# A fused spectral filter and state-space kernel: weight rows loaded twice by one transfer, and a new order of work

## The chip, the cores and the metric

The kernel runs on one core of a Trainium2 chip. The metric is device time in microseconds (us), the median over runs; a second number, the span, is the time from the first to the last instruction of one profiled execution. Engines are named as in the profile: PE is the matrix engine (PEld its weight loads), DVE the vector engine, ACT the scalar engine, POOL the general-purpose engine. SP is a sequencer that here only issues transfers (DMAs); a transfer is carried out by 16 DMA engines.

## The reference, cut to what matters

```
g = sigmoid((x * gate_w).sum(-1))               # x: 2048 x 1024
X = rfft2(x);  X = X * (w_r + 1j * w_i)         # w: 2048 x 513 each
a = irfft2(X)                                   # the spectral half
dt = exp(log_dt);  Lb = exp(dt * Lambda)        # 1024 complex states
Bu = x @ (((Lb - 1) / Lambda)[:, None] * B).T
h[t] = Lb * h[t - 1] + Bu[t]                    # a scan over 2048 steps
b = 2 * Re(h @ C.T) + x * Dskip                 # the state-space half
out = g * a + (1 - g) * b
```

## The kernel before, in words

All transforms are matrix products. The work falls into five stages, and the products `psu` of the state-space half (512 matmuls of 128x512, line 774) are strewn between the spectral stages as filling.

1. **Start.** 16 row blocks of x are loaded (L340) and turned on PE (L375) into `xT`. `halves` adds and subtracts halves of xT on DVE into `xpm` (L393, L395).
2. **Stage 1**, 16 steps j. `fd` (L532) makes the transform along columns, ACT copies it to `X1` (L537); `s1` (L547, L548) makes half of the transform along rows, ACT copies it to `A1` (L551), and SP writes A1 to a scratch tensor in DRAM, `turn1` (L553). At most three A1 buffers exist, and one is free again when its write has landed.
3. **Stage 2**, 16 steps b. `s2w` reads `turn1` back in another order (`Bb`, L655), PE multiplies it by a small matrix (L665), ACT copies the result (L668). The weights for step b come straight from DRAM into `Z(b, 0)` and `Z(b, 1)`, real and imaginary, 128 partitions x 1024 each: 64 partitions are needed, and both halves of the partitions get the same 64 rows. So there are four weight transfers a step (L659), each of 64 partitions x 2 rows x 512 values. DVE multiplies in place (L670). Column 0 is special: POOL sets column 0 of Z(b, 1) to zero (L660) and ACT puts a corrected value into column 0 of Z(b, 0) (L672), made by `fixup` out of column 0 of stage 1 (a small transfer to DRAM and back, `Bcol`, L611). `is1` (L681, L682) is the inverse along rows; its result goes to the scratch tensor `turn2` (L686).
4. **Stage 3**, 16 steps bp. `is2` reads `turn2` back (`Cq`, L693) when all 16 writes have landed, `idft` (L716) finishes the inverse, and the gated result goes to DRAM (L722).
5. **Output**, 16 steps tb: `ps_y` (512 matmuls, L818, and 128 small ones, L825), DVE combines with the spectral half read back (L845), SP writes the result (L848).

Beside these, DVE rotates and scans the states (`rot`, L742 to L748, and L786); the tables for that come from ACT (`table`).

The weights live in two tensors, `wA` and `wB`, with room for four steps in all: the loads for step b + 4 wait until `is1` of step b has read its room. The first eight (real and imaginary of steps 0 to 3; 16 transfers before the change) are loaded long before stage 2.

**What sets the order.** Nothing in the program text is in its final order. Every operation is recorded with an engine, a key, a duration in us, and what it reads and writes (`plan.op`). `Plan.run` then walks through them with these durations: of the operations that could start next on an engine it takes the one of lowest key, and gives out buffers as it goes. What comes out is a fixed list for each engine, and each engine works through its list in order, waiting by semaphores. Keys and durations (the second argument of `pe`, `act`, `dve`, `pool`, and the arguments `us` and `issue` of `dma`) thus set only the order. All transfers of the spectral half are issued by SP, in its one list.

Transfers carry eight completion semaphores in rotation: in the built program each transfer waits, before it is issued, for the one issued eight places before it. So at most eight are under way.

Of the kernel before, what the change touches and what calls it, by code (L numbers as in the profile page):

```python
# [11 lines left out]
ACT = mybir.ActivationFunctionType  # L12
# [23 lines left out]
def _host_consts():  # L36
# [30 lines left out]
    uu = np.arange(64)[None, None, :]  # L67
# [178 lines left out]
def kernel(  # L246
# [81 lines left out]
    KX = [0.0, 6.0, 10.0, 14.0]  # L328
    A2 = nc.scalar.activation

# [8 lines left out]
    for r in range(16):  # L339
        dma(r, 0.68, lambda r=r: nc.sync.dma_start(out=xn.t[:, r, :], in_=x[P * r:P * (r + 1), :]), w=[(xn, r)])  # L340
# [9 lines left out]
    dma(16.1, 2.6, lambda: nc.sync.dma_start(out=G_all, in_=cst["G"].rearrange("p d k -> p (d k)")), w=[("G",)])  # L350
    for i in range(2):
        dma(16.2, 2.0, lambda i=i: nc.sync.dma_start(out=TF_sb[i].t, in_=cst["TF"][:, 8 * i:8 * (i + 1)]), w=[(TF_sb[i],)])
    dma(16.3, 1.0, lambda: nc.sync.dma_start(out=TK_sb, in_=cst["TK"]), w=[("TK",)])
# [28 lines left out]
    def turn_x(c):  # L382
        for q in range(4):
            r = 4 * c + q
            turn(KX[c] + q, lambda r=r: xn.t[:, r, :], (xn, r), lambda c=c, q=q: xT[c][:, :, P * q:P * (q + 1)],
                 ("xT", c, q), q % 2)
# [4 lines left out]
    def halves(c):  # L391
        lo, hi = xT[c][:, 0:4, :], xT[c][:, 4:8, :]
        dve(KX[c] + 8, 1.22, lambda: nc.vector.tensor_add(out=xpm.t[:, 0, :, TC * c:TC * (c + 1)], in0=lo, in1=hi),  # L393
            r=xT_of(c), w=[(xpm, c, 0)])
        dve(KX[c] + 8.5, 1.22, lambda: nc.vector.tensor_sub(out=xpm.t[:, 1, :, TC * c:TC * (c + 1)], in0=lo, in1=hi),  # L395
            r=xT_of(c), w=[(xpm, c, 1)])
# [98 lines left out]
    def table(jb, key):  # L495
        tt = tile_of([P, 2, TC], FP32, "tt", "tt")
        tf = tile_of([P, 2, TC], FP32, "tf", "tf")
        cs = tile_of([P, 2, TC], BF16, "cs", "cs")
        kk, rr = lambda: tt.t[:, 0, :], lambda: tt.t[:, 1, :]
        sn_f, cs_f = lambda: tf.t[:, 0, :], lambda: tf.t[:, 1, :]  # L500
        at = lambda v: v[:, jb:jb + 1]
        act(key, 0.72, lambda: A2(out=kk(), in_=tau_f, func=ACT.Identity, scale=at(thn), bias=MAGIC),
            r=[("tau",), ("tht0",)], w=[(tt, 0)])
        act(key, 0.63, lambda: A2(out=kk(), in_=kk(), func=ACT.Identity, bias=-MAGIC), r=[(tt, 0)], w=[(tt, 0)])
        dve(key, 0.75, lambda: nc.vector.scalar_tensor_tensor(out=rr(), in0=tau_f, scalar=at(thn), in1=kk(), op0=ALU.mult,
                                                             op1=ALU.subtract), r=[("tau",), ("tht0",), (tt, 0)], w=[(tt, 1)])
# [34 lines left out]
    def s1(j, X1, key):  # L541
# [11 lines left out]
        dma(key, 0.68, lambda: nc.sync.dma_start(out=turn1_dram[j], in_=A1.t), r=[(A1,)], w=[("t1", j)])  # L553
# [3 lines left out]
    W_v = [w.rearrange("(q b h) k -> b q h k", b=16, h=2) for w in (A_w_r, A_w_i)]  # L557
# [4 lines left out]
    Bcol, Qz = fx.tile([P, 2, 16], BF16, name="Bcol"), fx.tile([P, 2, 16], BF16, name="Qz")  # L562
# [40 lines left out]
    def fixup(key):  # L603
# [4 lines left out]
        for c in range(2):  # L608
            def f(c=c):
                with nc.allow_non_contiguous_dma(reason="tiny corner turn"):  # L610
                    nc.sync.dma_start(out=Bcol[:, c, :], in_=col0_v[c])  # L611
            dma(key, 0.4, f, r=[("col0",)], w=[("Bcol", c)])
# [40 lines left out]
    def s2w(b, key):  # L653
        Bb = tile_of([P, 2, K], BF16, "Bb", "Bb")
        dma(key - 6, 0.84, lambda: nc.sync.dma_start(out=Bb.t, in_=t1_v[b]), r=[("t1", j) for j in range(16)], w=[(Bb,)])  # L655
        wr = (home(b), b % 2)
        for i in range(2):
            for c in range(2):
                dma(key - 6, 0.5, lambda i=i, c=c: nc.sync.dma_start(out=Z(b, i)[64 * c:64 * (c + 1)], in_=W_v[i][b][:, :, 0:K]), w=[wr + (i, c)])  # L659
        pool(key - 4, 0.1, lambda: nc.gpsimd.memset(Z(b, 1)[:, :, 0:1], 0.0), w=[wr + (1, 0), wr + (1, 1)])  # L660
# [8 lines left out]
        for i in range(2):  # L669
            dve(key, 0.69, lambda i=i: nc.vector.tensor_mul(out=Z(b, i), in0=X2.t, in1=Z(b, i)),  # L670
                r=[(X2,)], w=[wr + (i, 0), wr + (i, 1)])
        act(key + 1, 0.2, lambda: nc.scalar.copy(out=Z(b, 0)[:, :, 0], in_=Qz.rearrange("p o b -> p (o b)")[:, 2 * b:2 * b + 2]),  # L672
            r=[("Qz",)], w=[wr + (0, 0), wr + (0, 1)])

    def is1(b, key):
# [7 lines left out]
        pe(key, 4 * U, f, r=[(home(b), b % 2, i, c) for i in range(2) for c in range(2)] + [(MI_sb[b // 8],)], w=[(psc,)])  # L683
        C1 = tile_of([P, 2, K], BF16, "C1", "C1")
        act(key, 1.01, lambda: nc.scalar.copy(out=C1.t, in_=psc.t), r=[(psc,)], w=[(C1,)])  # L685
        dma(key, 0.86, lambda: nc.sync.dma_start(out=turn2_dram[2 * b:2 * b + 2].rearrange("h p k -> p h k"), in_=C1.t), r=[(C1,)], w=[("t2", b)])  # L686

    t2_v = turn2_dram.rearrange("b (r g i) k -> i (b r) g k", r=4, g=2)
    ga_v = ga_dram.rearrange("(p b) n -> p b n", b=16)

    def is2(bp, key):
        Cq = tile_of([P, 2, K], BF16, "Cq", "Cq")
        dma(key - 6, 0.86, lambda: nc.sync.dma_start(out=Cq.t, in_=t2_v[bp]), r=[("t2", b) for b in range(16)], w=[(Cq,)])  # L693
# [14 lines left out]
    def idft(bp, ZT, key):  # L708
# [13 lines left out]
        dma(key, 0.75, lambda: nc.sync.dma_start(out=ga_v[:, bp, :], in_=eo.t.rearrange("p h k -> p (h k)")), r=[(eo,)], w=[("ga", bp)])  # L722
# [3 lines left out]
    def load_CT(n, key):  # L726
        pc, ri = divmod(n, 2)
        dma(key, 3.0, lambda: nc.sync.dma_start_transpose(
            out=CT[pc].t[:, ri], in_=(B_C_re, B_C_im)[ri][:, 2 * P * pc:2 * P * (pc + 1)]), r=[("step", 2 * n, 0)], w=[(CT[pc], ri)], issue=2.4)
# [28 lines left out]
    def load_BT(jb, key):  # L758
        BTb[jb] = tile_of([P, 2, 8, P], BF16, "BTs", "bt")
        for ri, src in enumerate((B_B_re, B_B_im)):  # L760
            dma(key, 1.45, lambda ri=ri, src=src: nc.sync.dma_start_transpose(
                out=BTb[jb].t[:, ri], in_=src[P * jb:P * (jb + 1), :]), w=[(BTb[jb], ri)], issue=1.28)
# [47 lines left out]
    def yout(tb, key, diag):  # L810
# [12 lines left out]
        def f():  # L823
# [5 lines left out]
        dma(key - 6, 0.75, lambda: nc.sync.dma_start(out=eo.t.rearrange("p h k -> p (h k)"), in_=ga_dram[P * tb:P * (tb + 1), :]),  # L829
            r=[("ga", bp) for bp in range(16)], w=[(eo,)])  # L830
# [20 lines left out]
    K_T0 = 9.21  # L851
    K_TB = 7.38
    K_D = 16.61
    K_O = 42.27
    K_TAB0 = 19.63
    K_TAB = 4.93
    K_F0 = 21.64
    K_F = 1.92
    K_W0 = 56.75
    K_W = 1.73  # L860
    K_WI = 1.97
    K_I0 = 14.79
# [19 lines left out]
    def turns_of(lo, hi):  # L882
        for p, (jb, pr) in list(enumerate(turns))[lo:hi]:
            if pr == 0:
                tabs[jb] = table(jb, K_TAB0 if jb == 0 else KB(p, 0) - K_TAB)
                if jb:
                    load_BT(jb, KB(max(p - 2, 0), 0) + 2)
            carries[jb] = bu(jb, pr, tabs[jb], carries.get(jb), (KB(p, 0), KB(p, 1)), KD(p))
            if pr == 0:
                rot_out(jb, 0, 1, KD(p) + K_O)  # L890
                rot_out(jb, 1, 1, 400 + 3 * jb)
            else:
                rot_out(jb, 2, 2, 430 + 3 * jb)
# [11 lines left out]
    dma(130, 1.4, lambda: nc.sync.dma_start(out=G_all[:, 0:4 * K], in_=cst["Gi"].rearrange("p r k -> p (r k)")), w=[("G",)])  # L905
# [15 lines left out]
    for tb in range(16):  # L921
        yout(tb, 400 + 7 * tb, diag)
# [32 lines left out]
```

## Time and profile before

| | |
|---|---|
| median of 3 runs | 351.77 us (351.68 to 352.96) |
| profiled execution, its own time | 352.5 us |
| its span | 350.7 us, PE clock granted 0.995 |
| PE busy | 331.2 us (94%), 1917 matmuls |
| DVE busy | 293.7 us (84%) |
| ACT busy | 193.5 us (55%) |
| POOL busy | 21.9 us (6%) |
| transfers | 55.77 MB, mean 159 GB/s |

A page of the profile gives busy time of each engine, the same in 40 slices of the span, the transfers by queue, the chain of work that ended last, and the costliest groups of instructions. A group line reads: line, engine, operation, output <- inputs, shape, count | busy us, mean ns of one | idle time of the engine before them, and who ended it. A timeline row reads: start, duration, engine, line, operation. In the transfer section, a queue's line gives packets, MB, and the time that the packets took as a share of 16 engines' time; the completion notes are counted among the packets.

### The profile page before, as it was taken

Reading aid. Unit: us, or ns where it says so; the run is one execution under the profiler, and the core shown is the slowest. Engines: PE = TensorE matmul, PEld = TensorE weight load, DVE = VectorE, ACT = ScalarE, POOL = GpSimd, SP = SyncE. Lnnn points to the kernel's source line nnn. Section 1 sums busy time; section 2 is a strip of 40 time slices with the busy share of each in tenths; the row PEclk is TensorE's granted clock in tenths of the full one; section 3 lists DMA queues with packets and bytes.
Section 4 is the critical chain, followed back from the end, with each engine's and each line's share of the span. In section 5 each row is a group of like instructions: output and inputs, shape, how many; then the busy total and the mean of one; then the engine's idle time right before and its main releaser. Section 6 shows DMA issues by size and latency. Waiting matters only on the chain.

```text
span 350.7 us, 5296 instructions
## 1 busy us (share of the span) xinstructions
PE 331.2 (94%) x1917; PEld 172.9 (49%) x1917; DVE 293.7 (84%) x476; ACT 193.5 (55%) x270; POOL 21.9 (6%) x63
## 2 busy tenths in 40 slices
PE   5999999999997797799899999999999999999995
PEld 4655554555553343344345766654544454444542
DVE  2979999899999787899899999999999999622331
ACT  3897999999997768777649997940000000000000
POOL 1080000000004600000000000000000000000000
PEclk9999999999999899999999999999999999999999
DMA  7998870461175868999997999985233104100001
GB/s 247 309 318 67 211 206 32 92 181 62 60 178 154 240 140 232 247 247 249 230 249 201 249 254 260 232 250 179 90 97 116 60 32 149 60 32 30 30 32 60
DMA packets 69346, 55.77 MB, mean 159 GB/s; under 512 B 39364, under 2 KB 56004, under 8 KB 69192
## 3 DMA queue, kind: packets, MB, share of 16 engines
q1 hardware_dynamic: 69048, 55.40, 58.0%
q0 software_dynamic: 192, 0.02, 1.7%
q8 instruction: 15, 0.25, 0.3%
q14 instruction: 11, 0.09, 0.1%
q10 hardware_dynamic: 80, 0.01, 0.0%
HBM read 30.75 MB, written 16.79 MB: 136 GB/s over the span
## 4 chain that ended last, share of the span: by engine, by line
PE 58%; DVE 16%; ACT 10%; DMA 9%; SPq 4%; issue 2%; DVEq 0%; POOL 0%; POOLq 0%; ACTq 0%
PE ps_y L818 32%; PE psu L774 13%; DVE h L786 5%; PE ps_id L716 3%; PE ps_fd L532 3%; DMA wB<-in_A_w_r_dram 3%; DMA xn<-in_A_x_dram 2%; PE ps_y L825 2%; DVE su L742 2%; ACT u L777 2%; PE pt L375 2%; SPq L659 2%; DMA h<-turn_scratch 1%; DVE wB L670 1%; ACT X L537 1%
## 5 line engine op out<-in xcount | busy, mean ns | idle before, releaser
L774 PE MATMUL psu<-xT,BTs 128*128 128x512 bf16 x512 | 117.0, 379 | 1.5 <-ACT h L685 1.2
L818 PE MATMUL ps_y<-CT,h 128*128 128x512 bf16 x512 | 113.7, 379 | 0.0
L774 PEld LDWEIGHTS <-BTs 128*128 128x128 bf16 x512 | 49.7, 98 | 59.0 <-issue 2.1
L818 PEld LDWEIGHTS <-h 128*128 128x128 bf16 x512 | 49.3, 98 | 56.6 <-DVE h L746 0.6
L786 DVE TENSOR_TENSOR_SCAN h<-r_sb,carry,u 128x512 bf16<-128x512 f32 x48 | 59.6, 1271 | 0.1
L845 DVE SCALAR_TENSOR_TENSOR o<-ps_y,omg,ga 128x1024 bf16<-128x1024 f32 (+1 forms) x17 | 20.6, 1219 | 32.2 <-PE ps_y L825 32.2
L777 ACT CAST u<-psu 128x1024 bf16<-128x1024 f32 x32 | 32.5, 1017 | 7.8 <-PE psu L774 4.7
L532 PE MATMUL ps_fd<-G_all,xpm 128*128 128x512 bf16 x128 | 30.1, 379 | 0.5 <-ACT A L551 0.5
L532 PEld LDWEIGHTS <-xpm 128*128 128x128 bf16 x128 | 18.6, 146 | 10.4 <-issue 0.7
L537 ACT CAST X<-ps_fd 128x1024 bf16<-128x1024 f32 x16 | 21.5, 1342 | 0.1
L742 DVE TENSOR_TENSOR su<-h,pn 128x1024 bf16<-128x1024 bf16 (+1 forms) x24 | 20.7, 863 | 0.2
L743 DVE TENSOR_TENSOR h<-h,pn 128x1024 bf16<-128x1024 bf16 (+1 forms) x24 | 20.7, 862 | 0.1
L742 DVE TENSOR_TENSOR su<-u,cs 128x2048 bf16<-128x2048 bf16 x16 | 19.4, 1214 | 0.3
L743 DVE TENSOR_TENSOR u<-u,cs 128x2048 bf16<-128x2048 bf16 x16 | 19.5, 1219 | 0.2
L786 DVE TENSOR_TENSOR_SCAN h<-r_sb,u 128x512 bf16<-128x512 f32 x16 | 19.1, 1212 | 0.0
L685 ACT CAST h<-ps_is 128x1024 bf16<-128x1024 f32 x16 | 16.2, 1016 | 2.4 <-PE ps_is L682 1.3
L670 DVE TENSOR_TENSOR wA<-h,wA 128x1024 bf16<-128x1024 bf16 x16 | 10.8, 695 | 7.2 <-ACT h L668 2.6
L551 ACT CAST A<-ps_s 128x1024 bf16<-128x1024 f32 x16 | 16.6, 1037 | 0.0
L668 ACT CAST h<-ps_s 128x1024 bf16<-128x1024 f32 x16 | 16.0, 1022 | 0.3 <-DMA turn_scratch<-h 0.3
L721 ACT ACTIVATE eo<-ps_id,gA 128x1024 bf16<-128x1024 f32 x12 | 13.4, 1153 | 1.4 <-PE ps_id L716 1.4
L716 PE MATMUL ps_id<-G_all,ZT 128*128 128x256 bf16 x104 | 13.0, 273 | 1.0 <-ACT ZT L704 1.0
L375 PE MATMUL pt<-ident,xn 128*128 128x128 bf16 x128 | 10.0, 243 | 4.0 <-DMA xn<-in_A_x_dram 3.9
(160 smaller groups left out, 397.6 us busy)
## 6 DMA issues: line engine op xcount, KB each, us to landing
xn<-in_A_x_dram SPq DMA_DIRECT2D x16, 256.0 KB, 5.3
turn_scratch<-A SPq DMA_DIRECT2D x16, 256.0 KB, 2.7
h<-turn_scratch SPq DMA_DIRECT2D x16, 256.0 KB, 4.1
turn_scratch<-h SPq DMA_DIRECT2D x16, 256.0 KB, 3.2
out_dram<-o SPq DMA_DIRECT2D x15, 256.0 KB, 2.0
ga_scratch<-eo SPq DMA_DIRECT2D x12, 256.0 KB, 2.8
eoc<-ga_scratch SPq DMA_DIRECT2D x12, 256.0 KB, 4.2
Cq<-turn_scratch SPq DMA_DIRECT2D x11, 256.0 KB, 4.3
```

What stands on the lines that cost most here:

```text
L375: nc.tensor.transpose(out=pt.t[:, j8, :], in_=src()[:, P * j8:P * (j8 + 1)], identity=ident)
L532: mm(pf.t[:, par].rearrange("p c k -> p (c k)"), lhsT=xA[:, par, db, j, :], rhs=G_sb[:, db, par, :], start=(db == 0), stop=(db == 3))
L537: act(key, 1.3, lambda: nc.scalar.copy(out=X1.t.rearrange("p c (k r) -> p r c k", r=2), in_=pf.t), r=[(pf, 0), (pf, 1)], w=[(X1,)])
L551: act(key, 1.01, lambda: nc.scalar.copy(out=A1.t, in_=psa.t), r=[(psa,)], w=[(A1,)])
L716: mm(pz.t[:, at, :], lhsT=ZT.t[:, 2 * par + half, c, :], rhs=Gi_sb[:, par, half, c, :], start=(half == 0), stop=(half == 1))
L742: dve(key, w, lambda: nc.vector.tensor_mul(out=sv(), in0=src()[:, ::-1], in1=bc(1)), r=sitem + [titem(1)], w=[(su,)])
L743: dve(key, w, lambda: nc.vector.tensor_mul(out=dst(), in0=src(), in1=bc(0)), r=sitem + [titem(0)], w=ditem)
L774: mm(psu.t[:, ri, :], lhsT=BT.t[:, ri, db, :], rhs=xT[c][:, db, :], start=(db == 0), stop=(db == 7))
L777: act(kb[cc], 1.01, lambda cc=cc, psu=psu: nc.scalar.copy(out=u.t[:, :, cc, :], in_=psu.t), r=[(psu, 0), (psu, 1)], w=ui(cc))
L786: dve(kd, 1.25, lambda cc=cc, ri=ri, carry=carry: nc.vector.tensor_tensor_scan(out=g()[:, ri, cc, :], data0=rb, data1=u.t[:, ri, cc, :], i ...
L818: mm(psy.t[:, 512 * dh:512 * (dh + 1)], lhsT=hbuf[jb // 4].t[:, jb % 4, ri, P * tb:P * (tb + 1)], rhs=CT[pc].t[:, ri, jb % 2, 512 * dh:512 ...
L845: dve(key - 1, 0.2 + 1.07e-3 * (b - a), lambda a=a, b=b: nc.vector.scalar_tensor_tensor(out=o.t[:, a:b], in0=psy.t[:, a:b], scalar=og, in1 ...
```

## The change

The numbers behind the names below are this diff's own lines.

1. **Weight loads.** The two halves of the partitions are filled by one transfer: the source is given a leading dimension of 2 with step 0 (`[:, None].to_broadcast`). Each of the 64 rows of the source is now two whole neighbouring weight rows, 2 x 513 values (2052 bytes), and the room for it grows by 2 values. `Z` reads 512 of each 513. Two transfers a step instead of four. In the built program the source pattern of one is 2 (step 0) x 64 x 1026 values, where it was 64 x 2 x 512; the destination is 128 partitions x 1026 values, where it was 64 x 2 x 512.
2. **Column 0.** `Qz` holds for every step the corrected value and a zero beside it, so one ACT copy fills column 0 of Z(b, 0) and Z(b, 1); the 16 POOL memsets go, one larger one is added.
3. **Turn buffer in read order.** `MI`'s columns are permuted, so that the two rows which a partition of `Cq` reads from `turn2` lie side by side: one run of 2048 bytes instead of two of 1024.
4. **Constant loads.** The load of the inverse table `Gi` comes after `Qz`; the second `MI` load names `Bcol` among its reads, which at that place of the program text orders the Bcol loads after it in the plan.
5. **Durations and keys.** Planned durations of transfers grow, and all keys change, so that the lists of all engines are new.

```diff
-    uu = np.arange(64)[None, None, :]
+    uu = np.arange(64).reshape(2, 2, 16).transpose(0, 2, 1).reshape(1, 1, 64)
...
-    KX = [0.0, 6.0, 10.0, 14.0]
+    K_T0 = -26.99
+    K_TB = 21.89
...
+    K_FIX = -256.65
...
+    K_GATE = 154.0
+    KX = lambda c: K_XP * (c > 0) + K_XS * max(c - 1, 0)
...
-    dma(16.1, 2.6, lambda: nc.sync.dma_start(out=G_all, in_=cst["G"].rearrange("p d k -> p (d k)")), w=[("G",)])
+    dma(16.1, 4.0, lambda: nc.sync.dma_start(out=G_all, in_=cst["G"].rearrange("p d k -> p (d k)")), w=[("G",)])
...
-    W_v = [w.rearrange("(q b h) k -> b q h k", b=16, h=2) for w in (A_w_r, A_w_i)]
+    W_v = [w.rearrange("(q b h) k -> b q (h k)", b=16, h=2)[:, None].to_broadcast([16, 2, 64, 2 * (K + 1)]) for w in (A_w_r, A_w_i)]
...
-    Bcol, Qz = fx.tile([P, 2, 16], BF16, name="Bcol"), fx.tile([P, 2, 16], BF16, name="Qz")
+    Bcol, Qz = fx.tile([P, 2, 16], BF16, name="Bcol"), fx.tile([P, 16, 2, 2], BF16, name="Qz")
...
-        act(key, 0.2, lambda: nc.scalar.copy(out=Qz, in_=qps.t), r=[(qps,)], w=[("Qz",)])
+        pool(60, 0.2, lambda: nc.gpsimd.memset(Qz[:, :, 1, :], 0.0), w=[("Qz", 1)])
+        act(key, 0.2, lambda: nc.scalar.copy(out=Qz[:, :, 0, :], in_=qps.t.rearrange("p o b -> p (o b)").rearrange("p (b h) -> p b h", h=2)),
+            r=[(qps,), ("Qz", 1)], w=[("Qz",)])
...
-    wA = tile_of([P, 4, 2, K], BF16, "wA", "b8")
-    wB = tile_of([P, 4, 2, K], BF16, "wB", "b8")
+    wA = tile_of([P, 4, 2 * (K + 1)], BF16, "wA", "b8")
+    wB = tile_of([P, 4, 2 * (K + 1)], BF16, "wB", "b8")
...
-        dma(30 + 16 * i, 2.0, lambda i=i: nc.sync.dma_start(out=MI_sb[i].t, in_=cst["MI"][:, 16 * i:16 * (i + 1)]), w=[(MI_sb[i],)])
+        dma(30 + 16 * i, 3.0, lambda i=i: nc.sync.dma_start(out=MI_sb[i].t, in_=cst["MI"][:, 16 * i:16 * (i + 1)]),
+            r=[("Bcol", 1)] if i else [], w=[(MI_sb[i],)])
...
-    Z = lambda b, i: home(b).t[:, 2 * (b % 2) + i]
+    Zs = lambda b: home(b).t.rearrange("p n (h k) -> p n h k", h=2)[:, 2 * (b % 2):2 * (b % 2) + 2, :, 0:K]
+    Z = lambda b, i: Zs(b)[:, i]
...
-        dma(key - 6, 0.84, lambda: nc.sync.dma_start(out=Bb.t, in_=t1_v[b]), r=[("t1", j) for j in range(16)], w=[(Bb,)])
+        dma(key - K_DM, 1.0, lambda: nc.sync.dma_start(out=Bb.t, in_=t1_v[b]), r=[("t1", j) for j in range(16)], w=[(Bb,)], issue=0.49)
...
-            for c in range(2):
-                dma(key - 6, 0.5, lambda i=i, c=c: nc.sync.dma_start(out=Z(b, i)[64 * c:64 * (c + 1)], in_=W_v[i][b][:, :, 0:K]), w=[wr + (i, c)])
-        pool(key - 4, 0.1, lambda: nc.gpsimd.memset(Z(b, 1)[:, :, 0:1], 0.0), w=[wr + (1, 0), wr + (1, 1)])
+            dma(key - K_DM, 1.05, lambda i=i: nc.sync.dma_start(out=home(b).t[:, 2 * (b % 2) + i], in_=W_v[i][b]), w=[wr + (i,)], issue=0.5)
...
-        act(key + 1, 0.2, lambda: nc.scalar.copy(out=Z(b, 0)[:, :, 0], in_=Qz.rearrange("p o b -> p (o b)")[:, 2 * b:2 * b + 2]),
-            r=[("Qz",)], w=[wr + (0, 0), wr + (0, 1)])
+        act(key + 1, 0.2, lambda: nc.scalar.copy(out=Zs(b)[:, :, :, 0], in_=Qz[:, b]),
+            r=[("Qz",)], w=[wr + (0,), wr + (1,)])
...
-    t2_v = turn2_dram.rearrange("b (r g i) k -> i (b r) g k", r=4, g=2)
+    t2_v = turn2_dram.rearrange("b (r i g) k -> i (b r) g k", r=4, g=2)
...
-    dma(130, 1.4, lambda: nc.sync.dma_start(out=G_all[:, 0:4 * K], in_=cst["Gi"].rearrange("p r k -> p (r k)")), w=[("G",)])
+    dma(130, 2.0, lambda: nc.sync.dma_start(out=G_all[:, 0:4 * K], in_=cst["Gi"].rearrange("p r k -> p (r k)")), r=[("Qz",)], w=[("G",)])
...
-        yout(tb, 400 + 7 * tb, diag)
+        yout(tb, K_Y + K_YS * tb, diag)
```

More of the change, by code (lines that the diff above doesn't have):

```diff
@@ L327 @@
     U = 0.216
-    KX = [0.0, 6.0, 10.0, 14.0]
     A2 = nc.scalar.activation
+    K_T0 = -26.99
+    K_TB = 21.89
+    K_D = 126.57
+    K_O = 123.58
+    K_TAB0 = 58.67
+    K_TAB = -32.79
+    K_F0 = 35.7
+    K_F = 1.39
+    K_W0 = 35.52
+    K_W = 11.39
+    K_WI = -13.97
+    K_I0 = -209.45
+    K_I = 1.64
+    K_ID = -35.06
+    K_CT = 86.06
+    K_FIX = -256.65
+    K_R1 = 370.74
+    K_R2 = 785.78
+    K_RS = 117.7
+    K_Y = 801.27
+    K_YS = 99.96
+    K_H = -11.1
+    K_XP = -24.71
+    K_XS = 25.92
+    K_TP = -96.07
+    K_DM = 60.83
+    K_BT = 29.4
+    K_GATE = 154.0
+    KX = lambda c: K_XP * (c > 0) + K_XS * max(c - 1, 0)
     vec8 = tile_of([8, 5, P], BF16, "vec8", "tt")
@@ L339 @@
     for r in range(16):
-        dma(r, 0.68, lambda r=r: nc.sync.dma_start(out=xn.t[:, r, :], in_=x[P * r:P * (r + 1), :]), w=[(xn, r)])
+        dma(r, 0.8, lambda r=r: nc.sync.dma_start(out=xn.t[:, r, :], in_=x[P * r:P * (r + 1), :]), w=[(xn, r)])
         if r == 3:
@@ L349 @@
     TK_sb = cpool.tile([P, 9, P], BF16, name="TK_sb")
-    dma(16.1, 2.6, lambda: nc.sync.dma_start(out=G_all, in_=cst["G"].rearrange("p d k -> p (d k)")), w=[("G",)])
+    dma(16.1, 4.0, lambda: nc.sync.dma_start(out=G_all, in_=cst["G"].rearrange("p d k -> p (d k)")), w=[("G",)])
     for i in range(2):
-        dma(16.2, 2.0, lambda i=i: nc.sync.dma_start(out=TF_sb[i].t, in_=cst["TF"][:, 8 * i:8 * (i + 1)]), w=[(TF_sb[i],)])
-    dma(16.3, 1.0, lambda: nc.sync.dma_start(out=TK_sb, in_=cst["TK"]), w=[("TK",)])
+        dma(16.2, 3.0, lambda i=i: nc.sync.dma_start(out=TF_sb[i].t, in_=cst["TF"][:, 8 * i:8 * (i + 1)]), w=[(TF_sb[i],)])
+    dma(16.3, 1.2, lambda: nc.sync.dma_start(out=TK_sb, in_=cst["TK"]), w=[("TK",)])
     Kc, Ks, Kns, JJ, J0, RF, RI = [TK_sb[:, i, :] for i in range(7)]
@@ L384, in turn_x @@
             r = 4 * c + q
-            turn(KX[c] + q, lambda r=r: xn.t[:, r, :], (xn, r), lambda c=c, q=q: xT[c][:, :, P * q:P * (q + 1)],
+            turn(KX(c) + q, lambda r=r: xn.t[:, r, :], (xn, r), lambda c=c, q=q: xT[c][:, :, P * q:P * (q + 1)],
                  ("xT", c, q), q % 2)
@@ L611, in f @@
                     nc.sync.dma_start(out=Bcol[:, c, :], in_=col0_v[c])
-            dma(key, 0.4, f, r=[("col0",)], w=[("Bcol", c)])
+            dma(key, 1.2, f, r=[("col0",)], w=[("Bcol", c)], issue=0.64)
         zps = psum([P, 2, 16], "zps")
@@ L682, in f @@
                 mm(psc.t[:, h, :], lhsT=at(64), rhs=Z(b, 1)[:, h, :], start=False, stop=True)
-        pe(key, 4 * U, f, r=[(home(b), b % 2, i, c) for i in range(2) for c in range(2)] + [(MI_sb[b // 8],)], w=[(psc,)])
+        pe(key, 4 * U, f, r=[(home(b), b % 2, i) for i in range(2)] + [(MI_sb[b // 8],)], w=[(psc,)])
         C1 = tile_of([P, 2, K], BF16, "C1", "C1")
         act(key, 1.01, lambda: nc.scalar.copy(out=C1.t, in_=psc.t), r=[(psc,)], w=[(C1,)])
-        dma(key, 0.86, lambda: nc.sync.dma_start(out=turn2_dram[2 * b:2 * b + 2].rearrange("h p k -> p h k"), in_=C1.t), r=[(C1,)], w=[("t2", b)])
-    t2_v = turn2_dram.rearrange("b (r g i) k -> i (b r) g k", r=4, g=2)
+        dma(key, 1.05, lambda: nc.sync.dma_start(out=turn2_dram[2 * b:2 * b + 2].rearrange("h p k -> p h k"), in_=C1.t), r=[(C1,)], w=[("t2", b)], issue=0.61)
+    t2_v = turn2_dram.rearrange("b (r i g) k -> i (b r) g k", r=4, g=2)
     ga_v = ga_dram.rearrange("(p b) n -> p b n", b=16)
@@ L692, in is2 @@
         Cq = tile_of([P, 2, K], BF16, "Cq", "Cq")
-        dma(key - 6, 0.86, lambda: nc.sync.dma_start(out=Cq.t, in_=t2_v[bp]), r=[("t2", b) for b in range(16)], w=[(Cq,)])
+        dma(key - K_DM, 0.95, lambda: nc.sync.dma_start(out=Cq.t, in_=t2_v[bp]), r=[("t2", b) for b in range(16)], w=[(Cq,)], issue=0.49)
         psz = psum([P, 4, 2, P], "ps_is2")
@@ L721, in idft @@
         act(key, 1.11, lambda: A2(out=eo.t, in_=pz.t, func=ACT.Copy, scale=gA[:, bp:bp + 1]), r=[(pz, 0), (pz, 1), ("gA",)], w=[(eo,)])
-        dma(key, 0.75, lambda: nc.sync.dma_start(out=ga_v[:, bp, :], in_=eo.t.rearrange("p h k -> p (h k)")), r=[(eo,)], w=[("ga", bp)])
+        dma(key, 0.9, lambda: nc.sync.dma_start(out=ga_v[:, bp, :], in_=eo.t.rearrange("p h k -> p (h k)")), r=[(eo,)], w=[("ga", bp)], issue=0.5)
     CT = {pc: tile_of([P, 2, 2, D], BF16, "CT", "b8") for pc in range(4)}
@@ L728, in load_CT @@
         dma(key, 3.0, lambda: nc.sync.dma_start_transpose(
-            out=CT[pc].t[:, ri], in_=(B_C_re, B_C_im)[ri][:, 2 * P * pc:2 * P * (pc + 1)]), r=[("step", 2 * n, 0)], w=[(CT[pc], ri)], issue=2.4)
+            out=CT[pc].t[:, ri], in_=(B_C_re, B_C_im)[ri][:, 2 * P * pc:2 * P * (pc + 1)]), r=[("step", 2 * n, 0)], w=[(CT[pc], ri)], issue=3.4)
     hbuf = [tile_of([P, 4, 2, S], BF16, "h", "b32") for _ in range(2)]
@@ L761, in load_BT @@
             dma(key, 1.45, lambda ri=ri, src=src: nc.sync.dma_start_transpose(
-                out=BTb[jb].t[:, ri], in_=src[P * jb:P * (jb + 1), :]), w=[(BTb[jb], ri)], issue=1.28)
+                out=BTb[jb].t[:, ri], in_=src[P * jb:P * (jb + 1), :]), w=[(BTb[jb], ri)], issue=1.36)
     def bu(jb, pr, cs, carry, kb, kd):
@@ L828, in yout @@
         eo = tile_of([P, 2, K], BF16, "eoc", "eoc")
-        dma(key - 6, 0.75, lambda: nc.sync.dma_start(out=eo.t.rearrange("p h k -> p (h k)"), in_=ga_dram[P * tb:P * (tb + 1), :]),
-            r=[("ga", bp) for bp in range(16)], w=[(eo,)])
+        dma(key - K_DM, 0.75, lambda: nc.sync.dma_start(out=eo.t.rearrange("p h k -> p (h k)"), in_=ga_dram[P * tb:P * (tb + 1), :]),
+            r=[("ga", bp) for bp in range(16)], w=[(eo,)], issue=0.48)
         pq = tile_of([P, 2, 2, K // 2], BF16, "pq", "pq")
```

39 lines of the change are left out of this document (11 added, 28 removed).

## The prediction

> **What bounds the kernel now.** I read the page first by engine, then the chain, the stretches, the waits, and at last single transfers. From the page:
>
> ```profile
> PE 331.2 (94%) x1917; PEld 172.9 (49%) x1917; DVE 293.7 (84%) x476; ACT 193.5 (55%) x270; POOL 21.9 (6%) x63
> DMA  7998870461175868999997999985233104100001
> ```
>
> ```profile
> PE 58%; DVE 16%; ACT 10%; DMA 9%; SPq 4%; issue 2%; DVEq 0%; POOL 0%; POOLq 0%; ACTq 0%
> ```
>
> PE is the bound: 331 of 350.7 us. Counted at the spacing of its matmuls' starts in full rows (0.216 us for 512 columns, 0.109 for 256, 0.056 for 128), PE's list is 322.8 us; the other 28 are its start (7.5), pauses, and the tail after its last matmul (4.2). The stretches show where it pauses (stage 1, junction, stage 2, stage 3, output):
>
> ```profile
> 60.00:112.00 52.00, 51.42 (x252) 26.69 (x250) 49.71 (x73) 48.73 (x73) 2.22 (x5) 1.00 0.42 117
> 112.00:127.50 15.50, 11.67 (x67) 4.85 (x67) 12.88 (x18) 9.86 (x18) 7.74 (x16) 0.89 0.67 180
> 127.50:177.80 50.30, 44.87 (x204) 19.68 (x203) 43.24 (x63) 38.73 (x55) 1.18 (x11) 1.00 0.97 239
> 177.80:232.00 54.20, 52.75 (x399) 33.01 (x397) 54.10 (x74) 45.63 (x56) 0.11 (x1) 1.00 0.97 244
> 232.00:350.70 118.70, 114.50 (x625) 55.43 (x623) 83.33 (x174) 0.46 (x1) 0.00 (x0) 1.00 0.24 79
> ```
>
> The second-last column is the DMA engines' busy share. PE loses 3.8 us at the junction and 5.4 in stage 2, and in stage 2 the DMA engines are at 0.97: that stage is where the transfers matter, and the weight loads are half of what it moves. SP issues them singly, 0.62 us each, without a pause:
>
> ```profile
> 127.65 1.30 SPq L659 DMA_DIRECT2D wA<-in_A_w_r_dram  x2
> 129.06 1.24 SPq L659 DMA_DIRECT2D wA<-in_A_w_i_dram  x2
> 130.39 0.55 SPq L686 DMA_DIRECT2D turn_scratch<-h  x1
> ```
>
> **How a transfer is dealt out.** The change rests on this. Three transfers stand alone in a window: an output write (128 rows of 2 KB), the five small `vec` loads (8 rows each, the only ones of their queue), and a write of `grow_f` (1 row). The lines give packets, MB and the share of 16 engines' time:
>
> ```profile
> q1 hardware_dynamic: 144, 0.26, 35.2%
> ```
>
> ```profile
> q10 hardware_dynamic: 80, 0.01, 0.0%
> ```
>
> ```profile
> q1 hardware_dynamic: 2, 0.00, 0.3%
> ```
>
> The first (window of 2 us) is 128 rows and 16 completion notes; the second, for five transfers, 8 rows and 8 notes each; the third 1 row and 1 note. One note comes per engine that took part: so 16, 8 and 1 engines, as many as the leading number of the pattern allows. The single row was not cut to use more. An engine works its rows off one after another: 35.2% of 2 us on 16 engines is 11.3 us, over 128 rows 88 ns per 2 KB row.
>
> The new weight load's source leads with 2 (step 0), its destination with 128 partitions. No transfer before has sides that differ so, so which side counts is not shown. I let the smaller one decide: an engine's share must be the same rows on both sides, and a cut through the leading numbers that fits both has two parts. Then each load runs on **two** engines, 64 rows of 2052 bytes each: 64 x 88 ns = **5.6 us**, where the four half-loads of a step now use all sixteen. The rows do not name the engines; I take the same two for every load, since the 16 engines of a full transfer need no choosing and nothing shows a rotation (rival C).
>
> [...]
>
> **The change part by part.**
>
> *Weight loads, the first eight.* They follow the loads of the transform tables:
>
> ```profile
> 18.66 0.91 SPq L352 DMA_DIRECT2D TF_sb<-c_TF  x2
> ```
>
> ```profile
> TF_sb<-c_TF SPq DMA_DIRECT2D x2, 768.0 KB, 10.7
> ```
>
> The two engines are free of TF at 18.7 + 10.7 = 29. Eight loads: 29 + 8 x 5.6 = 74. TK, two BT loads and the first turn write stand behind them on these two engines, some 5 us by their share of rows: that write lands at 79. There are three A1 buffers, so the fourth A1 copy waits for it. PE has by then done 48.8 us of its list, at 7.5 + 48.8 = 56, and stands until about 82.5 (copy 1.04, the next s1 and its copy). That is **+26 us**. The rest of stage 1 is 30.7 us of PE: 113.
>
> *Junction.* The new order has 48 psu matmuls (10.4 us) and the fixup (1.7) here, which cover the landing of the last write; the Gi load, whose 512 KB go ahead of that write now, comes later. First product of stage 2 at 126, `is1` of step 0 done at 137.5 (four short steps and their copies).
>
> *Weight loads, the other 24.* The first reload starts at 137.5 (127.65 in before). 24 x 5.6 = 134.4 us on the two engines, plus what else they carry meanwhile: 11 turn2 writes, 6 Bb and 3 BT loads, at 0.7 to 1.4 us each, with MI and Gi about 17 to 20. The last weights land at **291**. PE has some 75 us of list in these 154: it stands about 6 of each 12.7 us step. SP's relief of 24 issues counts for nothing then.
>
> *After that.* Multiply (0.70, L670), patch, `is1` 0.86: 294. Landing of the last turn2 write (2.7) and of Cq (4.3), and psu between them: 303. The new list has done 163.2 of its 322.8 by then, 159.6 are left; I add 2.6 for the idle of stage 3 as it is now: 465.5. DVE has 147 us left, which fits. Tail 4.2: span 470. The profiled execution took 352.5, 1.8 over its span; 0.7 over the median: 470 + 1.8 - 0.7 = **471 us**.
>
> *Column patch.* 16 POOL memsets (0.11 us) go, ACT copies stay 16. POOL is 6% busy and the memsets wait for loads, not the reverse: nothing. Uncovered it were 16 x 0.1. One copy now waits for both loads of a step; the multiply waits for both anyway.
>
> *Turn buffer in read order.* Cq's rows double to 2048 bytes: 128 packets for 256. In the trace a packet of 1 KB takes 46 ns, one of 2 KB 84, so 256 x 46 against 128 x 84 over 16 engines is 0.06 us a load: nothing, and less issue on SP (0.64 to about 0.5). MI's columns are permuted beforehand and cost nothing.
>
> *Constant loads and keys.* Gi (512 KB) and half of MI (768 KB) no longer run ahead of the last turn1 writes, whose landing took 6.1 us of waiting there; 0 to -5 us, inside the junction above. The gate loads come some 65 us later in SP's list, at about 293, and are read at 304. Keys alone: the new lists have the same matmuls; DVE must run 9 us ahead of PE at the output, and does now by about the same. Within 2 us either way, DVE's wait as the bound.
>
> **Rivals.**
>
> *A: faster.* The destination's 128 rows decide, and all 16 engines carry the loads. Then 24 issues of about 0.65 us leave SP (15.6 us of stage 2, where SP never rests), transfers run in longer packets, and the junction is 5 us shorter, its clock loss 1.5. PE's pauses of 9 in stages 2 and 3 shrink until DVE binds: DVE stood 25.8 us behind its own list at the output and goes to about 20 to 23, so PE goes to 11 to 14: 322.8 + 12.5 + 4.2 + 1.8 = **341** (340 to 343). It decides as soon as a load uses more than about 8 engines, or 1.4 us. For it: packets of 128 x 2 KB are a plain shape that every other transfer here has on one side. Against it: the three rows above. [...]
>
> *B: two engines, but stage 1 goes on.* If later transfers pass the eight loads on these engines, or the loads are spread, the 26 us of stage 1 are away: 471 - 26 = **445**. Speaks for it: the wait list has waits on a turn write of at most 6.1 us now, so nothing shows how deep a line gets.
>
> *C: two engines, but others each time.* 24 loads overlap eight deep, the mean load stays as now: 345 to **352**, a change that does nothing much. Against it there is only the simpler rule; single-row transfers are too short to show where they ran.
>
> **How the numbers follow.** Forecast with two engines, all at the same two: 0.87, of which B takes 0.08; A 0.10; C 0.03. The price of a row lies between 81 ns (shortest 2 KB packet) and 100 (an estimate: 88 and a seventh more, as 1 KB packets take 46 ns at the median and 62 at the mean in stage 2, a third more, in mixed company): a load 5.2 to 6.4 us, 32 of them -13 to +26, with the psu filling absorbing part at the low end. So 458 to 497 without B, 435 with B and cheap rows. A stall or clock loss in stage 2 (the PE clock was 0.89 at the junction now) may add 5 to 8: **435 to 505**. Outside it: A, C. A measurement of this kernel can tell about 0.5% from no change. Faster 0.11 (A and a third of C), same 0.01, slower 0.88 (forecast, B, the rest of C).
>
> **What would show it.** Right: weight loads take 10 us or more from issue to landing (4.0 to 4.7 now) with 130 packets each, 128 rows and 2 notes; the DMA share of stage 2 falls from 0.97 to 0.2 to 0.3 while PE is half idle, its waits (L711, and DVE L700) ended by DMA wA or wB; PE and ACT have a gap of 20 us or more at 56 to 82; the last weight lands at 285 to 300, and output lasts as long as now. Wrong: landing under 5 us, 144 packets a load, no gap at 56: then A.

## The result, and the profile after

The changed kernel takes **464.31 us** (462.76 to 466.08, 4 runs) beside 352.37 us for the kernel before (351.68 to 353.50, 4 runs): 1.317 times as long (95% interval 1.311 to 1.324). The forecast was 471 us, with a range of 435 to 505.

From the page of the changed kernel, busy time and the 40 slices (one slice is 11.5 us here):

```profile
span 460.7 us, 5153 instructions
PE 352.4 (76%) x1882; PEld 178.9 (39%) x1917; DVE 295.3 (64%) x476; ACT 194.7 (42%) x270; POOL 22.4 (5%) x48
PE   6999900999995544555765145999999999999995
PEclk9999955799999666777778668999999999999998
DMA  8962129352671112289221886899974112231101
```

PE has two holes: zeros at the sixth and seventh digit, and a long stretch at 1 to 7 from the thirteenth to the twenty-fifth. In both, the granted clock falls to 0.5 to 0.8. The DMA row shows mostly ones and twos in the long stretch, with some sixes to nines between (more on those near the end). The same in stretches (the columns are the stretch and its length, then busy us and count of PE, PEld, DVE, ACT and POOL, and at last PE clock, DMA share and GB/s):

```profile
52.00:80.00 28.00, 4.82 (x22) 2.72 (x22) 17.05 (x28) 3.47 (x5) 0.00 (x0) 0.62 0.60 96
140.00:292.00 152.00, 79.33 (x276) 30.16 (x281) 58.64 (x83) 55.86 (x80) 0.00 (x0) 0.73 0.48 88
350.00:460.70 110.70, 105.47 (x576) 51.87 (x584) 82.03 (x172) 0.00 (x0) 0.00 (x0) 0.99 0.18 64
```

What the engines wait for stands in three group lines of the same page. L700 is the multiply by the weights, and L565 is the copy of `fd`'s result to X1:

```profile
L700 DVE TENSOR_TENSOR wB<-h,wB 128x1024 bf16<-128x1024 bf16 x16 | 11.1, 709 | 47.1 <-DMA wB<-in_A_w_i_dram 25.0
L700 DVE TENSOR_TENSOR wA<-h,wA 128x1024 bf16<-128x1024 bf16 x16 | 11.0, 701 | 45.7 <-DMA wA<-in_A_w_r_dram 23.1
L565 ACT CAST X<-ps_fd 128x1024 bf16<-128x1024 f32 x16 | 21.3, 1329 | 26.7 <-DMA turn_scratch<-A 24.5
```

The kernel before had this for the multiply (of one of the two tensors):

```profile
L670 DVE TENSOR_TENSOR wA<-h,wA 128x1024 bf16<-128x1024 bf16 x16 | 10.8, 695 | 7.2 <-ACT h L668 2.6
```

So DVE now stands 93 us before the multiplies, for the weights, and ACT stands 24.5 us for a write to turn1 in stage 1.

The chain of work that ended last was PE, DVE and ACT before, with 9% of DMA. Now:

```profile
PE 53%; DMA 27%; SPq 10%; DVE 3%; ACT 3%; issue 2%; POOL 1%; ACTq 0%; DVEq 0%; POOLq 0%
```

**What a weight load takes.** Between 41 and 51 us the first eight loads have the DMA engines almost to themselves. The transfer view of that window:

```profile
DMA packets 239, 0.49 MB, mean 49 GB/s; under 512 B 4, under 2 KB 4, under 8 KB 238
q1 hardware_dynamic: 238, 0.48, 12.9%
```

12.9% of 16 engines is 2.06 engines. Four small packets are the completion notes of two loads that ended in the window, two each. The other 234 are rows of 2052 bytes: 117 for each of two engines in 10 us, 85.5 ns a row, so a load, 64 rows on each engine, takes 5.47 us. The two engines move 49 GB/s together. The trace also has the time of each note. The first eight loads landed at 38.0, 43.6, 48.9, 54.7, 60.0, 65.3, 70.8 and 76.2 us, 5.3 to 5.8 us apart.

**What it does to SP.** The prediction had later transfers wait in line on the two engines. The timeline of SP's queue shows a second line, in front of that one:

```profile
20.65 0.71 SPq L690 DMA_DIRECT2D wA<-in_A_w_r_dram  x1
21.41 0.89 SPq L690 DMA_DIRECT2D wA<-in_A_w_i_dram  x1
22.34 10.11 SPq L690 DMA_DIRECT2D wA<-in_A_w_r_dram  x1
32.50 7.62 SPq L690 DMA_DIRECT2D wA<-in_A_w_i_dram  x1
40.24 5.09 SPq L690 DMA_DIRECT2D wB<-in_A_w_r_dram  x1
45.37 5.64 SPq L690 DMA_DIRECT2D wB<-in_A_w_i_dram  x1
51.06 5.19 SPq L690 DMA_DIRECT2D wB<-in_A_w_r_dram  x1
56.29 3.65 SPq L690 DMA_DIRECT2D wB<-in_A_w_i_dram  x1
59.98 7.43 SPq L381 DMA_DIRECT2D TK_sb<-c_TK  x1
67.58 5.87 SPq L791 DMA_TRANSPOSE BTs<-in_B_B_re_dram  x1
73.50 3.27 SPq L791 DMA_TRANSPOSE BTs<-in_B_B_im_dram  x1
76.87 11.71 SPq L581 DMA_DIRECT2D turn_scratch<-A  x7
```

The second column is how long the issue lasts. Two issues take the usual 0.7 to 0.9 us; from the third on an issue lasts about as long as a load (3.7 to 5.6, the third and fourth longer: until 26.4 the TF loads run as well, and from 28 to 38 four small loads that POOL issues take 56% of the 16 DMA engines' time). SP is held in the issue itself. It isn't the wait for the transfer eight places before: for each of the eight loads that one had landed by 26.4. What inside the issue holds SP the trace does not show. Everything behind it in its one list is held with it: the first turn1 write is issued at 76.9.

Both lines exist. The load issued at 40.24 landed at 60.0, with three loads still ahead of it on the two engines when its issue began. And TK, whose issue ended at 67.4, had 112 of its 128 rows carried at 68 to 70 us; the other 16, the share of two engines, followed at 75 to 76, when the rows of the last load were through. PE stands meanwhile:

```profile
54.98 1.89 PE L560 MATMUL ps_fd<-G_all,xpm 128*128 128x512 bf16 x7
80.73 0.59 PE L575 MATMUL ps_s<-X,TF_sb 128*128 128x512 bf16 x1 [23.85 <-ACT Acol L580]
```

### The profile page after: what moved, and what is told of

It is laid out like the page before. It is cut to its first block, busy times and chain, and to the rows that moved or that the text cites. A ratio compares the mean times of both kernels' runs of the same rounds, so it can differ in the third digit from the quotient of the medians.

```text
span 460.7 us, 5153 instructions
## 1 busy us (share of the span) xinstructions
PE 352.4 (76%) x1882; PEld 178.9 (39%) x1917; DVE 295.3 (64%) x476; ACT 194.7 (42%) x270; POOL 22.4 (5%) x48
## 4 chain that ended last, share of the span: by engine, by line
PE 53%; DMA 27%; SPq 10%; DVE 3%; ACT 3%; issue 2%; POOL 1%; ACTq 0%; DVEq 0%; POOLq 0%
PE ps_y L848 20%; PE psu L804 16%; DMA wB<-in_A_w_i_dram 11%; DMA wA<-in_A_w_i_dram 8%; PE ps_fd L560 5%; DMA turn_scratch<-h 5%; SPq L791 4%; SPq L690 4%; PE ps_id L746 3%; PE pt L403 2%; SPq L381 2%; PE ps_y L855 2%; PE ps_s L575 1%; DMA ga_scratch<-G_all 1%; PE ps_s L576 1%
## 5 line engine op out<-in xcount | busy, mean ns | idle before, releaser
L804 PE MATMUL psu<-xT,BTs 128*128 128x512 bf16 x497 | 127.0, 406 | 1.9 <-issue 0.7
L848 PE MATMUL ps_y<-CT,h 128*128 128x512 bf16 x499 | 111.9, 379 | 0.7
L804 PEld LDWEIGHTS <-BTs 128*128 128x128 bf16 x512 | 53.0, 104 | 68.9 <-issue 21.0
L700 DVE TENSOR_TENSOR wB<-h,wB 128x1024 bf16<-128x1024 bf16 x16 | 11.1, 709 | 47.1 <-DMA wB<-in_A_w_i_dram 25.0
L700 DVE TENSOR_TENSOR wA<-h,wA 128x1024 bf16<-128x1024 bf16 x16 | 11.0, 701 | 45.7 <-DMA wA<-in_A_w_r_dram 23.1
L711 PE MATMUL ps_is<-wB,MI_sb 128*128 128x512 bf16 x16 | 8.3, 522 | 36.7 <-ACT wB L702 36.7
L711 PE MATMUL ps_is<-wA,MI_sb 128*128 128x512 bf16 x15 | 8.2, 545 | 35.2 <-ACT wA L702 35.1
L712 PEld LDWEIGHTS <-MI_sb 128*128 128x128 bf16 x32 | 3.7, 117 | 74.3 <-issue 73.3
L565 ACT CAST X<-ps_fd 128x1024 bf16<-128x1024 f32 x16 | 21.3, 1329 | 26.7 <-DMA turn_scratch<-A 24.5
L560 PE MATMUL ps_fd<-G_all,xpm 128*128 128x512 bf16 x125 | 31.5, 395 | 0.1
L575 PE MATMUL ps_s<-X,TF_sb 128*128 128x512 bf16 x32 | 12.8, 401 | 23.9 <-ACT Acol L580 23.9
L533 DVE SCALAR_TENSOR_TENSOR tt<-tau_f,tht,tt 128x512 f32<-128x512 f32 x8 | 6.0, 748 | 27.3 <-ACT tt L532 27.3
```

The costliest lines, as they stand in the source:

```text
L560: mm(pf.t[:, par].rearrange("p c k -> p (c k)"), lhsT=xA[:, par, db, j, :], rhs=G_sb[:, db, par, :], start=(db == 0), stop=(db == 3))
L565: act(key, 1.3, lambda: nc.scalar.copy(out=X1.t.rearrange("p c (k r) -> p r c k", r=2), in_=pf.t), r=[(pf, 0), (pf, 1)], w=[(X1,)])
L804: mm(psu.t[:, ri, :], lhsT=BT.t[:, ri, db, :], rhs=xT[c][:, db, :], start=(db == 0), stop=(db == 7))
L848: mm(psy.t[:, 512 * dh:512 * (dh + 1)], lhsT=hbuf[jb // 4].t[:, jb % 4, ri, P * tb:P * (tb + 1)], rhs=CT[pc].t[:, ri, jb % 2, 512 * dh:512 ...
```

## The experiments

The theory: the pattern's leading 2 gives a load two of the 16 DMA engines. The rivals: the shape of the rows (2052 bytes, read twice) is slow; the new order is to blame; the other parts cost time as well. The runs were spread over three chips, so each line below has its own comparison with the kernel before, on the same chip.

| kernel | us | ratio to before (95% interval) |
|---|---|---|
| halves, 64 rows each (e1) | 343.35 | 0.970 (0.966 to 0.974) |
| leading 2, two different rows (e2) | 463.32 | 1.310 (1.306 to 1.314) |
| first eight loads in halves (e3) | 435.60 | 1.232 (1.228 to 1.236) |
| reloads in halves (e3b) | 369.59 | 1.047 (1.042 to 1.052) |
| copies in the inner loop (e4) | 341.33; again 341.15 | 0.966 (0.962 to 0.969); 0.966 (0.963 to 0.970) |
| the same, cut 62 and 2 (e6) | 464.65 | 1.315 (1.310 to 1.320) |
| before, with the leading-2 load (e5) | 483.13 | 1.368 (1.363 to 1.373) |
| before, with the inner-loop load (e9) | 349.43 | 0.988 (0.985 to 0.992) |
| e4 without part 4, constant loads (e7) | 345.85 | 0.981 (0.977 to 0.985) |
| e4 without part 3, turn buffer (e8) | 341.31 | 0.967 (0.963 to 0.971) |
| e4 without part 2, column patch (e10) | 344.48 | 0.976 (0.972 to 0.980) |

**e1: no broadcast.**

```diff
-nc.sync.dma_start(out=home(b).t[:, 2 * (b % 2) + i], in_=W_v[i][b])
+for c in range(2):
+    nc.sync.dma_start(out=home(b).t[64 * c:64 * (c + 1), 2 * (b % 2) + i], in_=W_h[i][b])   # W_h: 64 x 1026
```

> Each weight load is split into its two halves of 64 partitions, both from the same 64 source rows of 1026 values: two plain transfers with a leading 64 on both sides in place of one with a leading 2. Rows, bytes, and the order of the work stay. Theory (the leading 2 confines a load to two engines): all 16 engines carry it again, the gap at 52 to 80 and the pauses in stage 2 go, 343 to 352 us, the 32 more issues on SP costing a little. Rival (the rows are to blame: 2052 bytes, not a multiple of 512, crossing lines, or the same rows read twice): nothing changes, 455 to 470.

343.35 us: the whole loss is gone, with the same rows of 2052 bytes read twice. Row length and repeated reading are out. Each of the two transfers now has 16 completion notes, where the load had two.

**e2: the leading 2 without the repeat.**

```diff
-in_=W_v[i][b]                                # step 0 between the copies
+in_=W_h[i][b // 2 * 2:b // 2 * 2 + 2]        # 2 x 64 x 1026, step of one row
```

> The load keeps its leading 2, but with a real step: the second half of the partitions gets the rows of the neighbouring step instead of the same rows again, so the weights of one half are those of another step and the output is not the reference's; the work is the same on every engine. Theory (the leading number): same as the changed kernel, 458 to 470 us. Rival (the step of 0, or reading the same DRAM rows twice, is slow): 341 to 352.

463.32 us, as the changed kernel, and SP's issues are held again: 8.5 and 10.1 us for the third and fourth, 5.1 to 5.4 for the next three. It is the 2, not the step of 0.

**e4: copies in the inner loop.** One transfer still fills all 128 partitions, but now row q, copy c goes to partition 2q + c. (In the cut, A and B stand for the two halves of the old MI, and the comments for the change of RF.)

```diff
-W_v = [w.rearrange("(q b h) k -> b q (h k)", ...)[:, None].to_broadcast([16, 2, 64, 2 * (K + 1)]) ...]
+W_v = [w.rearrange("(q b h) k -> b q (h k)", ...)[:, :, None].to_broadcast([16, 64, 2, 2 * (K + 1)]) ...]
...
-MI = np.concatenate([A, B], axis=0)                    # RF.reshape(P, P)
+MI = np.stack([A, B], axis=1).reshape(P, 32, 192)      # RF.transpose(0, 1, 2, 4, 5, 3).reshape(P, P)
```

> Still one transfer per load that reads the same 64 rows twice with a step of 0, but the loop over the two copies is the inner one: the source pattern is 64 x 2 (step 0) x 1026, the destination 128 partitions, so that copy c of row q lands in partition 2q + c. The columns of RF, the rows of MI and the selection matrices of the column fixup are permuted to fit; every engine's list is that of the changed kernel. Theory (smaller leading number decides): 64 and 128 lead, all 16 engines carry the load, 338 to 347 us, faster than before, as rival A of the prediction had it. Rival (repeat or row shape): 455 to 470.

341.33 us, **faster than the kernel before by 3.4%**, with the same lists on all engines as the changed kernel at 464. The first issues in its timeline (from the second run of it):

```profile
20.30 0.65 SPq L690 DMA_DIRECT2D wA<-in_A_w_r_dram  x1
20.99 0.68 SPq L690 DMA_DIRECT2D wA<-in_A_w_i_dram  x1
21.71 0.66 SPq L690 DMA_DIRECT2D wA<-in_A_w_r_dram  x1
```

No issue is held, where the third one took 10.1 us above, and each load has 16 completion notes.

**e6: no small number in front.** As e4, each load cut in two (W_h is here e4's source of 64 x 2 x 1026):

```diff
+for lo, hi in ((0, 62), (62, 64)):
+    nc.sync.dma_start(out=home(b).t[2 * lo:2 * hi, 2 * (b % 2) + i], in_=W_h[i][b, lo:hi])   # 62 x 2 x 1026 -> 124
```

> The interleaved kernel (copies in the inner loop), with each load cut into two transfers of 62 and 2 source rows, so that 62 and 124 lead on the two sides of the big one. No pattern leads with a small number any more where the bytes are. Reading 1 (as many engines as the leading number allows, up to 16): 341 to 350 us, near the halves kernel. [...]

464.65 us. Its window from 41 to 51 us:

```profile
q1 hardware_dynamic: 236, 0.47, 12.8%
```

The same two engines' worth (12.8% of 16 is 2.05), and 8 completion notes: two for each of four transfers. So the count is not "as many as the leading number allows": for 62 that would be 16, and reading 1 with its 341 to 350 us is out. Measured by pairs of leading numbers: 2 and 128 gave two engines, 62 and 124 two, 64 and 64 (e1) sixteen, 64 and 128 (e4) sixteen. Each count divides both numbers of its pair, and 62 and 124 have no common divisor between 2 and 31. How a count is picked beyond these four pairs, no run shows.

**e3 and e3b: the two holes one at a time.**

```diff
+if b < 4:        # e3; b >= 4 in e3b
+    for c in range(2):
+        nc.sync.dma_start(out=home(b).t[64 * c:64 * (c + 1), 2 * (b % 2) + i], in_=W_h[i][b])
+else:
     nc.sync.dma_start(out=home(b).t[:, 2 * (b % 2) + i], in_=W_v[i][b])
```

> Only the first eight loads (steps 0 to 3) are split into halves of 64 partitions; the 24 reloads keep the leading 2. Theory (the stall of PE at 52 to 80 comes from the turn1 writes queued behind the eight loads): that stall of 26.7 us goes whole and the rest moves up, 434 to 442 us. Rival (the stall has another cause, or the reloads are limited by something that does not move up): 455 to 466.

> The other half of the first-eight run: the first eight loads keep the leading 2, the 24 reloads are split into halves of 64 partitions on 16 engines. Theory (the stall of stage 1 and the stretching of stage 2 are two separate losses that add): the halves kernel (343) and the stall of 26.7 us, 366 to 372 us; with the first-eight run the two losses then make up the whole 121 us. Rival (a delay in stage 1 is made good later, since PE waits for DVE in stage 2): under 360.

e3 took 435.60, e3b 369.59. Against e1 (343.35) the first eight loads cost 369.59 - 343.35 = 26.2 us, the 24 reloads 435.60 - 343.35 = 92.3; together 118.5 of the 121.0 between e1 and the changed kernel. The two losses add to within 3 us (e3b ran on another chip than e1 and e3, with the kernel before at 354.02 beside it and 353.96 beside them); next to nothing of the first is made good later.

**e5 and e9: the load alone, in the order of before.** Rooms of 2 x 513 values and the load of the changed kernel (e5), or that of e4 (e9); nothing else.

> The kernel before, with the changed kernel's weight load alone (source leading with 2, rows of 2052 bytes, one transfer for both halves of the partitions); column patch, turn buffer, constant loads and keys stay as before. Theory (the load is the whole loss): as slow as the changed kernel or a little slower, since the order before has a longer junction, 462 to 478 us. Rival (the loss needs the new order, for instance because the new order has the loads wait at a worse place): under 440.

483.13 us: the load alone does it, and more than expected. ACT's longest wait on a turn1 write is 31.8 us here (24.5 in the changed kernel), and the first reload goes out at 161.0 (136.4):

```profile
ACT A L551 <- DMA turn_scratch<-A: 31.8, 1, 31.8
```

So the changed kernel's other parts give back 19 us of the load's loss. Its stall is 7 us shorter and its first reload 25 us earlier; which part of the change does that was not tried with this load.

> The kernel before, with the interleaved load alone (one transfer, 64 rows x 2 copies, 16 engines); everything else stays. Against the interleaved kernel in the new order (341) it tells what the load is worth by itself and what the other parts bring. Theory (issues on SP and the shorter stage 2 give about half, junction and order the rest): 344 to 350 us. Rival 1 (the load is worth everything): 340 to 343. Rival 2 (the load is worth nothing, all comes from the order): 351 to 354.

349.43 us: the load by itself is worth 3.9 us (353.3 for before in those runs), little over 1% but clear of the interval; the other parts of the change bring 8 (349.4 to 341.3, on two chips). The theory's range held, but not its halves. Junction and stage 2 of e9:

```profile
113.00:127.00 14.00, 9.60 (x49) 3.68 (x49) 12.12 (x16) 7.64 (x12) 8.84 (x16) 0.76 0.57 163
127.00:177.00 50.00, 48.14 (x221) 21.71 (x225) 45.58 (x66) 40.57 (x62) 1.28 (x12) 1.00 0.86 264
```

PE's idle time in stage 2 is 1.9 us in place of 5.4, as rival A had it. The load alone does not shorten the junction: PE is idle there for 4.4 us (3.8 before), and the first reload is issued at 130.6 (127.65 before).

**e7, e8, e10: the other parts, undone in e4 one by one** (partner: 341.15, on the same chip as e8 and e10; e7 ran on another).

```diff
-r=[("Bcol", 1)] if i else [], w=[(MI_sb[i],)])      # e7; also r=[("Qz",)] of the Gi load
+w=[(MI_sb[i],)])
-t2_v = ... "b (r i g) k -> i (b r) g k"             # e8; and MI's columns
+t2_v = ... "b (r g i) k -> i (b r) g k"
+pool(key - 4, 0.1, lambda: nc.gpsimd.memset(Z(b, 1)[:, :, 0:1], 0.0), w=[wr + (1,)])   # e10
-act(key + 1, 0.2, lambda: nc.scalar.copy(out=Zs(b)[:, :, :, 0], in_=Qz[:, b]), ...)
+act(key + 1, 0.2, lambda: nc.scalar.copy(out=Z(b, 0)[:, :, 0], in_=Qz[:, b, 0, :]), ...)
```

> The interleaved kernel once more, as the partner of the two runs beside it: 340.5 to 342.5 us.

> The interleaved kernel with part 3 of the change undone: MI's columns in their old order, and Cq read in two runs of 1024 bytes a partition in place of one of 2048; every engine's list is the same. Theory (the prediction's nothing: 0.06 us a load of DMA time and a shorter issue on SP, which has no work waiting there): within 1 us of its partner. Rival (issue and descriptors of Cq are on the path of stage 3): 2 us or more slower.

341.31, 0.2 us from its partner: the turn buffer brings nothing, as forecast.

> The interleaved kernel with part 2 of the change undone: a POOL memset for column 0 of Z(b, 1) in every step and an ACT copy for column 0 of Z(b, 0) alone; the 29 more operations shift the lists a little. Theory (the memsets are hidden): within 2 us of the partner, whichever way the shifted lists go. Rival (the memset sits between the load's landing and the multiply, and the wait chain of POOL delays the step): 3 us or more slower.

344.48, 3.3 us slower; the expectation of 2 failed. The memset itself is not it. The longest of DVE's waits for POOL between 100 and 240 us, of the view of waits:

```profile
DVE wA L701 <- POOL wA L691: 0.2, 1, 0.2
```

PE loses its time between 165 and 190 us, here e10 and then its partner:

```profile
165.00:190.00 25.00, 22.30 (x178) 13.96 (x177) 24.90 (x38) 21.96 (x31) 0.00 (x0) 1.00 0.82 218
```

```profile
165.00:190.00 25.00, 24.82 (x186) 15.32 (x185) 24.90 (x38) 23.05 (x34) 0.00 (x0) 1.00 1.01 219
```

DVE is busy alike; PE and ACT meet in another sequence there, because 16 more memsets made the planner put out other lists. In e10 PE runs 48 psu matmuls in a row from 165.05 on and then `is2` and `idft` without filling, waiting eight times from 177 to 188, 0.2 to 0.4 us each, for ACT. In its partner eight psu matmuls stand between most of these groups, and PE waits once. That the lists are the cause is what is left after the memset is out, and the sequence fits it; it was not tried by itself.

> The interleaved kernel with part 4 of the change undone: the Gi and second MI loads are free to run early again, as before; the lists of all engines change a little with it. Theory (the prediction's 0 to -5 us for this part): 341 to 346 us, with the last turn1 write landing later. Rival (part 4 does nothing once the loads use 16 engines): 340.5 to 342.

345.85, 4.7 us more than e4 (0.981 of before against 0.966, so 5 us by the ratios): within the expected 341 to 346, at the bound of the prediction's 0 to -5. But the reason given was wrong: only Gi runs early (issued at 81.8 against 104.7; the second MI load goes out at 86.1 against 85.1), the first Bb is issued at 91.5 against 90.6 and the first reload at 108.57 against 108.69. These times of the junction hardly move; PE falls behind after it:

```profile
115.00:125.00 10.00, 8.35 (x40) 3.70 (x38) 8.90 (x13) 9.18 (x14) 0.00 (x0) 1.00 1.03 353
```

```profile
115.00:125.00 10.00, 10.00 (x48) 4.54 (x47) 9.41 (x13) 9.87 (x16) 0.00 (x0) 1.00 1.03 363
```

(e7, then e4 again.) More is lost between 165 and 190 us, where e10 lost its time: PE is busy for 22.20 us in e7 against 24.82, and waits for ACT between `is2` and `idft` as in e10. So its lists differ too, and how much Gi's bytes and how much the lists do stays open.

## Why the prediction was right, point by point

- **Two engines, the same two each time.** Two is right, shown by e1, e2, e4, and by two notes a load with 2.06 engines busy. The trace does not name the engines. That they are the same two is read from the constant 49 GB/s: some three loads were under way at once, so rival C, other engines each time, would have raised that rate. The step "the smaller leading number decides" was right for 2 and 128 and wrong for 62 and 124, which gave two (e6).
- **5.6 us a load.** 5.47 measured; 32 loads, 4 us less.
- **The stall of stage 1, +26.** PE stood from 56.9 to 80.7 (forecast 56 to 82.5); by e3b it is worth 26.2, and rival B, where stage 1 goes on, is out. The place was right, the mechanism in part: there is a line on the two engines, as forecast, and one in SP's issue, which the forecast did not have. The first turn1 write landed at 79.3, against a forecast of 79, and some of that is luck: the TF loads were done at 26.4 and not at 29, but POOL's small loads, left out of the sum, held up the first weight load to 38.0. The buffer was another, too. It was not the fourth A1 copy that waited (it ran at 53.8) but the X1 copy after it, L565, for the landing of the first turn1 write.
- **Junction.** First reload at 136.4 (forecast 137.5).
- **The 24 reloads.** The last multiply of weights starts at 282.5, having waited 4.65 us for the landing; the forecast had the landing at 291. Of 146 us, 24 x 5.47 are 131, and 15 are left for other transfers and gaps; the forecast had 134 and 17 to 20 for other transfers. These two terms are the mis-sized ones, 7 of the 9 us that the landing came early; the earlier first reload is 1 more.
- **After it.** 282.5 to the end of the span at 460.7 is 178 us, the forecast's 291 to 470 was 179 (its sum 303 + 159.6 + 2.6 is 465.2, not 465.5, which changes nothing).
- **Issue to landing.** Forecast 10 us or more: the first eight loads took 17 to 27, with two notes each.
- **DMA share in stage 2.** Forecast 0.2 to 0.3, measured 0.48. Two full engines are 0.125. The packet records of 140 to 280 us show where the rest comes from: the 3541 packets of 256 bytes took 154 ns each in the mean, against 30 ns in stage 2 of before, 546 of some 1021 engine-us (the busy times of all engines added up). Their median is 18 ns in both; 76 of them, lasting up to 7.0 us, make 484 of the 546. I read these as packets that waited and were counted as busy; what they waited for, the records don't say.
- **Rival A's 341.** Its time for loads on all 16 engines was right (341.3 in e4), but its split was off: in the old order the load is worth 4 us, and the other parts bring 8. Column patch and keys were put at nothing and at 2 us, the constant loads at up to 5; undoing the patch moved the time by 3.3, undoing the constant loads by 4.7. In both runs part of it or all came with other lists, so the forecast probably sized the sensitivity to the order too small.

## What to carry to other kernels

Before trusting a broadcast or merged transfer, look at the first number of both sides of the pattern as the built program has it, and at what divides both: here 2 and 128 gave two engines, 62 and 124 gave two, 64 and 128 gave all sixteen, a difference of 123 us for the same bytes. Put the copies in the inner loop and permute the constants around it, and the merged load is a small gain (349.4 against 353.3 by itself; in the new order 341.3, against 343.4 with two halves). In a profile, such a transfer shows as few notes for many packets (2 for 128 rows), issue rows of 5 us on a queue that used to issue in 0.6, and, in a stretch where it runs alone, a DMA share of 0.13. Beside other transfers the share is higher and hides it (0.48 in stage 2).

## What the runs showed that was not expected

SP was held inside the issue from the third load on, so a few narrow transfers blocked loads and writes that had nothing to do with them, beyond the share that these had on the two engines. In e4 the same eight loads were issued in 6 us, each in 0.5 to 1.0.
